# A linear-attention plus SwiGLU block on one core: 384 instead of 512 tokens in the conventional part, preparation of the weights laid out anew

## The chip, the core and the metric

The kernel runs on one core of a Trainium2 chip. A core has TensorE (matmul, called PE; its weight loads are PEld), VectorE (DVE), ScalarE (ACT), GpSimd (POOL) and SyncE (SP, which issues DMAs here). They run side by side and wait for each other with semaphores. SBUF is the working memory, PSUM (eight banks of 512 fp32 columns per partition) takes what TensorE writes. The metric is the device time of one execution in microseconds (us).

## The reference

```python
x  = A_x                                   # [1, 2048, 512], bf16
xn = layernorm(x)                          # no gain, no bias, eps 1e-5
# A: linear attention, 32 heads of 16
q, k, v = split(xn @ wqkv)                 # wqkv [512, 1536]
phi = lambda t: where(t > 0, t + 1, exp(t)) + 1e-6
kv  = sum_s phi(k)_s v_s^T                 # per head, 16 x 16
z   = sum_s phi(k)_s
o   = (phi(q) kv) / (phi(q) z + 1e-6)
A   = o @ wo                               # wo [512, 512]
# B: SwiGLU
B   = (silu(xn @ w_gate) * (xn @ w_up)) @ w_down   # F = 1792
out = x + A + B
```

## The kernel before

Tokens lie in 16 tiles of 128. The program is written as a list of operations in an order set by hand: each `K.add(engine, ...)` appends one operation with the keys it reads and writes, waits are worked out from the keys, and every engine runs its own operations in the order of the list. Nothing is reordered at run time, so a late operation holds up all that stands behind it on its engine.

**Stage 1, to 48.7 us.** Normalisation, transposition of xn into xnT (by DMA, `dmat`, L412; tiles 0 to 3 by TensorE), the projections of q and k (`proj`, L431), phi, and G = xn^T phi(k) accumulated in banks 0 to 3 (`gacc`, L480). The order is the long text in `run`, whose words are a letter for a step and a tile number: D is `dmat`, q and k are projections. Behind it SP queues the loads of the gate, up, v, output and down weights. GpSimd then adds up z over 16 tiles (`z_add`, L497).

**Stage 2, conventional part, 48.7 to 74.7 us.** For the first `T0` = 512 tokens, 14 steps of gate and up (`gu`, L556): eight matmuls of 512 columns each, Silu on ScalarE (L564), the multiplication on VectorE (`hop`, L593). In step 2 the products of G with the v weights go in between (L605). Beside it the seven-product stage is prepared: the sum of squares of each weight matrix is bounded (`square` on ScalarE, L708 and, for w_down, `square_d`, L753; `top`, a maximum on VectorE, L714), turned into a power of two (`gather`, `total`, `scales`), with which `scale` multiplies the weights (ScalarE L800, GpSimd L801). `x_sum` and `w_sums` (both L808) form sums of blocks of xnT and of the weights in fp16.

**Stage 3, seven-product part, 74.7 to 154.0 us.** For the other 1536 tokens gate and up together are a product of 2 x 2 blocks, done with seven block products instead of eight (Winograd's form of Strassen's scheme). An iteration handles one of 14 blocks of 128 of F, for two halves q of `TS` = 384 columns: `prod` (L846) issues two matmuls per product and half; `seed` and `keep5` copy a bank (ScalarE, L856, L861); `gate` is Silu (L868); `u4` and `up22` combine (VectorE, L874, L879); `h22` (GpSimd, L883) and `h21` (VectorE, L889) write the result. `fill` puts matmuls of the conventional down projection of tiles 0 to 3 in between, 72 in all, FA and FB of them at two places of an iteration. Beside it go the scales and sums of the next weights, and per iteration one tile's division by the attention's denominator (`pz_mul`, `den_sum`, `den_turn`, `pq_mul`) and its transposition by DMA (`turn`).

**Stage 4, 154.0 us to the end.** The down projection and the attention output of 12 tiles in six pairs (`PAIRS`), again with seven products (`dprod`, L1083; `attn`, L1089), copies by `hcopy` (L1055), sums by `h_sum` (L1067), outputs by `dout` (L1115) and stores on SP.

Of the kernel before, what the change touches and what calls it, by code (L numbers as in the profile page):

```python
# [40 lines left out]
class _Program:  # L41
# [8 lines left out]
    def add(self, eng, fns, r=(), w=(), dma=False, a=()):  # L50
# [7 lines left out]
        for k in tuple(w) + tuple(a):  # L58
            if k in self.last_w:
                deps.add(self.last_w[k])  # L60
            deps |= self.readers.get(k, set())
        keep = []
        for d in deps:
            o = self.ops[d]
            if o["eng"] == eng and not o["dma"]:
# [52 lines left out]
def bass_parallel_sum__linear_attn_block__swiglu_ffn__prompt_kernel(nc, A_x, A_wqkv, A_wo, B_x, B_w_gate, B_w_up, B_w_down, out):  # L118
# [5 lines left out]
    with contextlib.ExitStack() as es:  # L124
# [17 lines left out]
        wg = sb("wg", [P, NDC, F], bf)  # L142
        wu = sb("wu", [P, NDC, F], bf)
# [38 lines left out]
        pqf = pq[:, :, :].rearrange("p a b -> p (a b)")  # L182
        wqf = wqkv[:, :, :].rearrange("p c f -> p (c f)").bitcast(f16)
# [18 lines left out]
        iw = sb("iw", [P, 2], f32)  # L202
        junks = [b_[:, :, :].rearrange("p a b -> p (a b)").bitcast(bf)[:, 0:F // 2] for b_ in (p5, c22)]
# [10 lines left out]
        banks = [E(nc.psum_tensor("pb%d" % i, [P, 512], f32)) for i in range(8)]  # L214
# [68 lines left out]

        blockmask(("maskt",), maskt[:, :], maskt[:, :].rearrange("p (a b) -> p a b", a=HPG), [[0, DH]])
# [128 lines left out]
        def dmat(t):  # L413
            K.add("sp", lambda e: e.dma_start_transpose(out=xnT[:, :, t * P:(t + 1) * P], in_=xn[:, t, :]),
                  r=[("xn", t)], w=[("xnT", t)], dma=True)

# [100 lines left out]
        def run(text):  # L517
# [11 lines left out]
            S6 m15 q10 x12 D14 s15 m12 k10 y10 s12 n10 k11 D0 x10 u10 R7 m10 q15 x11 s10 q11 m11 y15 L7 R6 s11  # L529
            D7 n15 k13 y11 u15 q13 n11 x13 L6 u11 D6 m13 q14 y13 s13 n13 q12 y14 u13 n14 k14 y12 u14 n12 q7  # L530
            x14 u12 m14 k7 y7 L1 s14 D1 n7 k6 x7 u0 m7 q6 u7 x6 s7 m6 G4 y6 s6 n6 G12 u2 G14 u6 u1 G6 u8 G10
            u3 G11 G15 G8 G13 G7
        """)
        fload("sp", "wg", wg, B_w_gate, 0)
        fload("sp", "wu", wu, B_w_up, 0)
        wload("sp", 2)
        woload("sp")

        for h in (1,):
            fload("sp", "wg", wg, B_w_gate, h)  # L540
            fload("sp", "wu", wu, B_w_up, h)
# [7 lines left out]
        def gu(j, extra=(), er=(), ew=()):  # L549
            C, fc = j // NFC, j % NFC  # L550
            n = (len(extra) + 7) // 8
            todo = list(extra)
            for b, w_, key in ((gb(j), wg, "wg"), (gb(j) + 1, wu, "wu")):
                fns = []
                for c in range(NDC):
                    fns.append(lambda e, c=c, b=b, w_=w_: e.matmul(  # L556
                        banks[b][:, :], w_[:, c, fc * P:(fc + 1) * P], xnT[:, c, C * 512:(C + 1) * 512],
# [4 lines left out]
                      r=sum([xkeys(t) for t in range(4 * C, 4 * C + 4)], []) + [(key, fc // 7), (key + "c", fc)] + list(er),  # L562
                      w=[B(b)] + list(ew))
            K.add("act", lambda e: e.activation(sil[:, j % 2, :], banks[gb(j)][:, :], ACT.Silu),  # L564
                  r=[B(gb(j))], w=[("sil", j % 2)])

        def h0(fc):
            return xn[:, 10 + fc, :] if fc < 6 else pk[:, 2 + fc, :]

        def h0key(fc):  # L570
            return ("xn", 10 + fc) if fc < 6 else ("pk", 2 + fc)

        HB = 2 * TB

        def hj(fc):
            if fc < 9:
                return hTf[:, fc * HB:(fc + 1) * HB]
            return xnf[:, (fc - 9) * HB:(fc - 8) * HB] if fc < 12 else pqf[:, (fc - 12) * HB:(fc - 11) * HB]

        def hjold(fc):  # L580
            if fc < 9:
                return ph1
            if fc < 12:
                return [("xn", t) for t in range(3 * (fc - 9), 3 * (fc - 8))]
            return [("pq", t) for t in range(3 * (fc - 12), 3 * (fc - 11))]

        def htile(t, fc):
            if t < 4:
                return h0(fc)[:, t * P:(t + 1) * P], h0key(fc)
            return hj(fc)[:, (t - 4) * P:(t - 3) * P], ("hj", fc, (t - 4) // 3)  # L590

        def hop(j):
            K.add("dve", lambda e: e.tensor_tensor(  # L593
                out=h0(j), in0=banks[gb(j) + 1][:, :], in1=sil[:, j % 2, :], op=ALU.mult),
                r=[B(gb(j) + 1), ("sil", j % 2)], w=[h0key(j)])
# [82 lines left out]
        def ounits(bank, t):  # L678
            out = []
            for fc in range(NFC):  # L680
# [3 lines left out]
                    start=(fc == 0 and t < 2), stop=(fc == NFC - 1 and t > 1))), [k_, ("wd", 7 * (fc // 7))], [B(bank)]))  # L684
# [10 lines left out]
        def oout(bank, t, home=None):  # L695
            dst = out_sb[:, t % 2, :] if home is None else home
            keys = [("ob", t % 2, 0), ("ob", t % 2, HD)] if home is None else [("ob", t)]
            K.add("dve", lambda e: e.tensor_tensor(out=dst, in0=banks[bank][:, :], in1=x_sb[:, t, :], op=ALU.add),
                  r=[B(bank)] + xk(t), w=keys, a=() if home is None else [("T", 4)])
# [37 lines left out]
        def scales(b):  # L737
# [6 lines left out]
                r=[B(b)], w=[B(b)])  # L744
            K.add("dve", lambda e: e.tensor_scalar(
                out=sw[:, :], in0=r_, scalar1=2.0 ** (SB - 65), scalar2=None, op0=ALU.mult), r=[B(b)], w=[("sw",)])
            K.add("dve", lambda e: e.tensor_scalar(
                out=iw[:, :], in0=e_, scalar1=2.0 ** (64 - SB), scalar2=None, op0=ALU.mult), r=[B(b)], w=[("iw",)])
            K.add("dve", lambda e: e.tensor_scalar(
                out=sx[:, :], in0=sw[:, 0:1], scalar1=2.0 ** SX, scalar2=None, op0=ALU.mult), r=[("sw",)], w=[("sx",)])  # L750
# [14 lines left out]
        def total_d(b):  # L765
# [4 lines left out]
        def scales_d(b):  # L770
# [583 lines left out]
```

## Time and profile before

| | us |
|---|---|
| three runs | 295.39, 200.62, 201.09 |
| median of them | 201.09 |
| profiled execution, its own time | 200.89 |
| its span, first to last instruction | 199.6 |

| engine | busy us | share of the span |
|---|---|---|
| TensorE | 195.1 | 98% |
| TensorE weight loads | 114.8 | 58% |
| VectorE | 170.5 | 85% |
| ScalarE | 153.6 | 77% |
| GpSimd | 122.3 | 61% |

The page gives busy time per engine, the chain of work that ended last, groups of instructions (line, engine, operation, written tile, read tiles, shape, count, then busy time, mean ns of one, and idle time before them with what ended it) and DMA queues. A line named in a group is that of the helper that issues it. Busy TensorE time is not peak time: matmuls overlap, so a matmul's pace is read from how many of them a stretch of the chain holds. The granted TensorE clock was 1.00 throughout.

### The profile page before, as it was taken

Reading aid. Unit: us, or ns where it says so; the run is one execution under the profiler, and the core shown is the slowest. Engines: PE = TensorE matmul, PEld = TensorE weight load, DVE = VectorE, ACT = ScalarE, POOL = GpSimd, SP = SyncE. Lnnn points to the kernel's source line nnn. Section 1 sums busy time; section 2 is a strip of 40 time slices with the busy share of each in tenths; the row PEclk is TensorE's granted clock in tenths of the full one; section 3 lists DMA queues with packets and bytes.
Section 4 is the critical chain, followed back from the end, with each engine's and each line's share of the span. In section 5 each row is a group of like instructions: output and inputs, shape, how many; then the busy total and the mean of one; then the engine's idle time right before and its main releaser. Section 6 shows DMA issues by size and latency. Waiting matters only on the chain.

```text
span 199.6 us, 3566 instructions
## 1 busy us (share of the span) xinstructions
PE 195.1 (98%) x1193; PEld 114.8 (58%) x1207; DVE 170.5 (85%) x339; ACT 153.6 (77%) x308; POOL 122.3 (61%) x150
## 2 busy tenths in 40 slices
PE   8899999999999999999999999999999999999995
PEld 2344444444544445555555555555555888888884
DVE  2999998894797798988888998887799999998866
ACT  3799887749889988689898988888989968475200
POOL 3687876799995544787677666768877004413220
DMA  6943243289990000011111221000210012132223
GB/s 180 355 122 81 57 87 73 50 282 364 375 295 3 0 3 0 0 28 31 26 26 26 53 56 23 4 0 7 45 34 0 3 39 66 30 79 66 45 69 118
DMA packets 28899, 15.97 MB, mean 80 GB/s; under 512 B 17232, under 2 KB 28880, under 8 KB 28880
## 3 DMA queue, kind: packets, MB, share of 16 engines
q1 hardware_dynamic: 28320, 15.28, 27.3%
q10 hardware_dynamic: 560, 0.46, 0.7%
q8 instruction: 9, 0.15, 0.3%
q14 instruction: 10, 0.08, 0.1%
HBM read 9.70 MB, written 2.10 MB: 59 GB/s over the span
## 4 chain that ended last, share of the span: by engine, by line
PE 94%; DVE 2%; DMA 2%; issue 1%; ACT 0%; POOL 0%; SPq 0%
PE pb L846 32%; PE pb L1083 16%; PE pb L431 13%; PE pb L556 12%; PE pb L480 7%; PE pb L682 6%; PE pb L1089 5%; PE pb L686 2%; DMA x_sb<-in_A_x_dram 2%; PE pb L605 1%; PE pb L674 0%; DVE pq L470 0%; PE pb L398 0%; POOL ef L459 0%; DVE stats L298 0%
## 5 line engine op out<-in xcount | busy, mean ns | idle before, releaser
L654 POOL TENSOR_TENSOR pq<-pq,rden 128x512 bf16<-128x512 bf16 x16 | 16.9, 1056 | 36.7 <-DVE rden L650 23.1
L868 ACT ACTIVATE zacc<-pb,iw 128x384 bf16<-128x384 f32 x56 | 31.3, 590 | 5.9 <-PE pb L846 4.7
L431 PE MATMUL pb<-wqkv,xnT 128*128 128x512 bf16 x110 | 25.1, 379 | 0.2
L846 PE MATMUL pb<-xnT,wg 128*128 128x384 bf16 x112 | 25.1, 326 | 0.0
L638 POOL TENSOR_TENSOR pz<-pq,zbc 128x512 f32<-128x512 bf16 x16 | 18.6, 1164 | 5.3 <-DVE ef L808 3.8
L883 POOL TENSOR_TENSOR hT<-c,zacc 128x384 bf16<-128x384 f32 x18 | 16.1, 915 | 6.0 <-DVE c L879 4.0
L459 POOL TENSOR_SCALAR ef<-ef 128x512 bf16<-128x512 bf16 x25 | 15.5, 620 | 5.8 <-ACT ef L452 5.6
L879 DVE TENSOR_TENSOR c<-pb,p 128x384 f32<-128x384 f32 x28 | 15.5, 555 | 4.1 <-PE pb L846 2.8
L431 PEld LDWEIGHTS pb<-wqkv,xnT 128*128 128x128 bf16 x112 | 10.9, 98 | 13.3 <-DVE pk L470 0.4
L452 ACT ACTIVATE ef<-pb 128x512 bf16<-128x512 f32 x25 | 14.8, 593 | 3.9 <-PE pb L431 3.9
L874 DVE TENSOR_TENSOR pb<-pb,p 128x384 f32<-128x384 f32 x28 | 15.3, 561 | 1.7 <-PE pb L846 0.9
L497 POOL TENSOR_TENSOR zacc<-zacc,pk 128x512 f32<-128x512 f32 x13 | 15.4, 1181 | 1.0
L856 ACT ACTIVATE pb<-pb 128x384 f32<-128x384 f32 x28 | 12.7, 473 | 3.8 <-PE pb L846 2.9
L846 PEld LDWEIGHTS pb<-xnT,wg 128*128 128x128 bf16 x112 | 10.6, 98 | 7.7 <-ACT pb L856 0.8
L556 PE MATMUL pb<-xnT,wg 128*128 128x512 bf16 x56 | 14.7, 379 | 0.0
L556 PE MATMUL pb<-xnT,wu 128*128 128x512 bf16 x53 | 14.3, 379 | 0.1
L846 PE MATMUL pb<-xnT,wqkv 128*128 128x384 bf16 x56 | 13.7, 326 | 0.0
L846 PE MATMUL pb<-GT,wqkv 128*128 128x384 f16 x56 | 13.7, 326 | 0.0
L846 PE MATMUL pb<-wo,wqkv 128*128 128x384 f16 x56 | 13.7, 326 | 0.0
L298 DVE BATCH_NORM_STATS2 stats<-x_sb 128x6 f32<-128x512 bf16 x16 | 10.8, 678 | 3.0 <-DMA x_sb<-in_A_x_dram 3.0
L1089 PE MATMUL pb<-M,pk 128*128 128x256 bf16 x96 | 13.4, 273 | 0.0
L480 PE MATMUL pb<-pk,xn 128*128 128x512 bf16 x55 | 12.5, 379 | 0.1
(210 smaller groups left out, 488.6 us busy)
## 6 DMA issues: line engine op xcount, KB each, us to landing
x_sb<-in_A_x_dram SPq DMA_DIRECT2D x14, 128.0 KB, 4.5
wg<-in_B_w_gate_dram SPq DMA_DIRECT2D x2, 896.0 KB, 8.3
wu<-in_B_w_up_dram SPq DMA_DIRECT2D x2, 896.0 KB, 9.6
wd<-in_B_w_down_dram SPq DMA_DIRECT2D x2, 896.0 KB, 13.7
out_dram<-out_sb SPq DMA_DIRECT2D x24, 64.0 KB, 1.6
wqkv<-in_A_wqkv_dram SPq DMA_DIRECT2D x3, 256.0 KB, 5.0
wqkv<-in_A_wqkv_dram SPq DMA_DIRECT2D x1, 512.0 KB, 9.0
wo<-in_A_wo_dram SPq DMA_DIRECT2D x1, 512.0 KB, 10.0
```

The source lines that it names most:

```text
L431: K.add("pe", [(lambda e, c=c: e.matmul(banks[b][:, :], src[:, c, t * P:(t + 1) * P], wqkv[:, c, col:col + D], start=(c == 0), stop=(c == ...
L459: K.add("pool", lambda e: e.tensor_scalar(out=buf, in0=buf, scalar1=top, scalar2=0.0, op0=ALU.min, op1=ALU.max), r=[bkey] + tkeys, w=[bkey])
L480: K.add("pe", [(lambda e, c=c: e.matmul(banks[c][:, :], src[:, t, c * P:(c + 1) * P], pk[:, t, :], start=first, stop=last)) for c in range ...
L556: fns.append(lambda e, c=c, b=b, w_=w_: e.matmul(banks[b][:, :], w_[:, c, fc * P:(fc + 1) * P], xnT[:, c, C * 512:(C + 1) * 512], start=(c ...
L638: K.add("pool", lambda e: e.tensor_tensor(out=pzh[i][:, :, 0:DH], in0=heads(pq[:, t, :]), in1=heads(zbc[:, :]), op=ALU.mult), r=[("pq", t) ...
L654: K.add("pool", lambda e: e.tensor_tensor(out=heads(pq[:, t, :]), in0=heads(pq[:, t, :]), in1=rden[:, i, :][:, :, None].broadcast_to([P, N ...
L846: K.add("pe", [(lambda e, c=c: e.matmul(banks[bank][:, 0:TS], L[i][:, c, :], R[i][:, c, ts], start=(start and c == 0), stop=(c == 1), skip ...
L868: K.add("act", lambda e: e.activation(sil4[:, n, :], bk(bank), ACT.Silu, scale=iw[:, 0:1]), r=[B(bank), ("iw",)], w=[("sil4", n), ("zacc", ...
L879: K.add("dve", lambda e: e.tensor_tensor(out=c22[:, q, :], in0=bk(b), in1=p5[:, q, :], op=ALU.add), r=[B(b), ("p5", q)], w=[("c22", q)])
L883: K.add("pool", lambda e: e.tensor_tensor(out=hj(fc)[:, TB + q * TS:TB + (q + 1) * TS], in0=c22[:, q, :], in1=sil4[:, 2 * q + 1, :], op=AL ...
L1083: K.add("pe", [(lambda e, k=k: e.matmul(split(banks[b][:, 0:HD]), L[:, k, :], cut[:, :, k * P:(k + 1) * P], start=(start and k == 0), stop ...
L1089: K.add("pe", [(lambda e, g=g: e.matmul(dk(b), pk[:, SLOT[t], g * P:(g + 1) * P], M[:, g, lo:lo + HD], start=False, stop=(g == NG - 1), sk ...
```

## The change

- `T0` is 384: the conventional part takes three tiles with matmuls of 384 columns; the seven-product part has 1664 tokens in halves of 416 columns. Buffers that lie in freed memory (`h0`, `hj`) move accordingly. Tile 3 goes through the seven-product gate and up, but its down projection stays among the 72 fill matmuls; its scale is undone by one more ScalarE copy on `rden` (in `den_turn`) and in `oout`.
- The first half of the gate weights is queued on SP behind the transposition of tile 14, the first half of the up weights behind that of tile 6; the transposition of tile 0 stands just ahead of that of tile 1. The second gate half comes first of the other loads, the second up half behind wo.
- The preparation is two texts in the manner of `run`: `AHEAD` (seven squares, one maximum, the G evictions, x_sum 1) before the first gate/up step, and `BESIDE`, by step 0 to 13 of the conventional part, and from 14 on by half iterations of the seven-product part. Three w_down squares stay beside the conventional part; five, and w_down's scale, are in the iterations. The scales of the first and third pair of up blocks move to ScalarE.
- The gate's factor is negative. All sums with gate weights become additions, so `w_sums` forms S0 and S2 with one VectorE instruction of 1024 columns (a repeated operand and a backward step over one joined tensor `wgu`), and the copies, `u4`, `up22` change sign.
- Banks of the two halves are (4, 2, 6) and (5, 3, 7). Fill matmuls per iteration come from a table `FILLS`.
- Token order of the divisions and the pairs is nearly the natural one. In the last pair the fourth product of the down projection is issued behind two attention parts instead of ahead of them.

```diff
-T0 = 512
+T0 = 384
-ORDER = (0, 1, 2, 3, 4, 5, 10, 11, 12, 13, 14, 15, 6, 7, 9, 8)
+ORDER = tuple(range(14)) + (15, 14)
-PAIRS = (10, 4, 12, 14, 6, 8)
+PAIRS = (4, 6, 8, 10, 12, 14)
...
         def dmat(t):
...
+            if t == LG:
+                fload("sp", "wg", wg, B_w_gate, 0)
+            if t == LU:
+                fload("sp", "wu", wu, B_w_up, 0)
...
-            S6 m15 q10 x12 D14 s15 m12 k10 y10 s12 n10 k11 D0 x10 u10 R7 m10 q15 x11 s10 q11 m11 y15 L7 R6 s11
+            S6 m15 q10 x12 D14 s15 m12 k10 y10 s12 n10 k11 x10 u10 R7 m10 q15 x11 s10 q11 m11 y15 L7 R6 s11
...
-            x14 u12 m14 k7 y7 L1 s14 D1 n7 k6 x7 u0 m7 q6 u7 x6 s7 m6 G4 y6 s6 n6 G12 u2 G14 u6 u1 G6 u8 G10
+            x14 u12 m14 k7 y7 L1 s14 D0 D1 n7 k6 x7 u0 m7 q6 u7 x6 s7 m6 G4 y6 s6 n6 G12 u2 G14 u6 u1 G6 u8 G10
...
-        fload("sp", "wg", wg, B_w_gate, 0)
-        fload("sp", "wu", wu, B_w_up, 0)
+        fload("sp", "wg", wg, B_w_gate, 1)
         wload("sp", 2)
         woload("sp")
-
-        for h in (1,):
-            fload("sp", "wg", wg, B_w_gate, h)
-            fload("sp", "wu", wu, B_w_up, h)
+        fload("sp", "wu", wu, B_w_up, 1)
...
+            if t == C0:
+                K.add("act", lambda e: e.activation(rden[:, i, :], rden[:, i, :], ACT.Copy, scale=sw[:, 1:2]),
+                      r=[("rden", i), ("sw",)], w=[("rden", i)])
...
             if part == 0:
-                tt("dve", S_[0], A21, A22, ALU.add, uk, [("S", n, 0)] + old)
-                tt("dve", S_[1], S_[0], A11, ALU.subtract, gk + [("S", n, 0)], [("S", n, 1)])
+                both = Sw[:, n, 0:3:2, :, :]
+                lhs = A21[:, None, :, :].broadcast_to([P, 2, 2, 2 * P])
+                tt("dve", both, lhs, wgu[:, :, cs].rearrange("p (x c) f -> p x c f", c=2)[:, 3::-3, :, :], ALU.add,
+                   gk + uk, [("S", n, 0), ("S", n, 2)] + old)
             else:
-                tt("dve", S_[2], A11, A21, ALU.subtract, gk + uk, [("S", n, 2)])
-                tt("dve", S_[3], A12, S_[1], ALU.subtract, gk + [("S", n, 1)], [("S", n, 3)])
-
-        GB = ((2, 3, 4), (5, 6, 7))
+                tt("dve", S_[1], S_[0], A11, ALU.add, gk + [("S", n, 0)], [("S", n, 1)])
+                tt("dve", S_[3], A12, S_[1], ALU.add, gk + [("S", n, 1)], [("S", n, 3)])
+
+        GB = ((4, 2, 6), (5, 3, 7))
...
+        AHEAD = "q130 q000 q110 q120 q030 t010 G00 q021 G30 q020 G21 G11 X1"
+        BESIDE = {0: "q101 t100", 2: "t001 q011 q131 k", 4: "t121 m0 m1 t031 d5", 6: "q111 u012 u045 u078 u101 u167 g m2", 8: "T C m3 X3 d1", 9: "a10", 11: "p00 W0 d7 W1 Z2", 12: "z0", 13: "X2 a12 z1 p11 p01 X4", 14: "d6 d3", 18: "d4", 21: "d0", 22: "d2", 27: "h", 28: "D e", 29: "s0", 30: "s1", 32: "s2 s3", 33: "s4 s5"}
...
-        FA, FB = 2, 3
-        DIV = {i: ORDER[i] for i in range(11)}
-        TURN = {11: (8, 9), 12: (10,)}
+        FILLS = ((3, 4), (2, 3), (1, 3), (3, 5), (1, 4), (1, 2), (0, 2), (2, 2), (1, 3), (1, 3), (1, 3), (1, 2), (3, 3), (6, 1))
+        DIV = {i + 0: ORDER[i] for i in range(11)}
...
         oout(1, 3, spare[1])
         dprod(p, 3, e, False)
-        dprod(p, 4, b, False)
         attn(p, 0, HD, e)
         dout(p, 0, HD, e)
         attn(p, 0, 0, a)
         dout(p, 0, 0, a)
+        dprod(p, 4, b, False)
         attn(p, 1, 0, b)
         dout(p, 1, 0, b)
```

In the two texts q is a square, t a maximum, G an eviction of G, X an x_sum, W a half of w_sums, a and p a scale on ScalarE or GpSimd, d a square of w_down, z a denominator product, Z the total of z; k, m, T, C, g, h, D, e, s and u are the small steps in between.

More of the change, by code (lines that the diff above doesn't have):

```diff
@@ L213, in bass_parallel_sum__linear_attn_block__swiglu_ffn__prompt_kernel @@
         sm = sb("sm", [P, 1], f32)
-        banks = [E(nc.psum_tensor("pb%d" % i, [P, 512], f32)) for i in range(8)]
+        psum = E(nc.psum_tensor("pb", [P, 8, 512], f32))
+        banks = [psum[:, i, :] for i in range(8)]
         def B(i):
@@ L561, in gu @@
                 K.add("pe", fns,
-                      r=sum([xkeys(t) for t in range(4 * C, 4 * C + 4)], []) + [(key, fc // 7), (key + "c", fc)] + list(er),
+                      r=sum([xkeys(t) for t in range(C0)], []) + [(key, fc // 7), (key + "c", fc)] + list(er),
                       w=[B(b)] + list(ew))
-            K.add("act", lambda e: e.activation(sil[:, j % 2, :], banks[gb(j)][:, :], ACT.Silu),
+            K.add("act", lambda e: e.activation(sil[:, j % 2, 0:T0], banks[gb(j)][:, 0:T0], ACT.Silu),
@@ L763, in gather_d, with total_d @@
                 r=[("as1",)], w=[("as1b",)])
-        def total_d(b):
+        where_d = []
+        def total_d():
+            where_d.append([b for b in (1, 0) if not busy.get(B(b))][0])
+            b = where_d[0]
             one = nc.const_aps.tensor(1.0, (P, P), bf)
@@ L898, in fill @@
                 K.add("pe", fn, r=r, w=w)
+                busy[w[0]] = after is None
                 if after is not None:
```

269 lines of the change are left out of this document (120 added, 149 removed).

## The prediction

> **What bounds the kernel now.** I read the page first (parts 1, 2 and 4), then busy time by stage, the groups by shape, the waits, and the timeline around the stage borders.
>
> ```profile
> span 199.6 us, 3566 instructions
> ...
> PE 195.1 (98%) x1193; PEld 114.8 (58%) x1207; DVE 170.5 (85%) x339; ACT 153.6 (77%) x308; POOL 122.3 (61%) x150
> ...
> PE 94%; DVE 2%; DMA 2%; issue 1%; ACT 0%; POOL 0%; SPq 0%
> ```
>
> TensorE is busy for 98% of the span and carries 94% of the chain that ended last. Busy is not yet peak, so I checked the pace: in the chain 21 matmuls of 512 columns take 4.53 us, 20 of 384 take 3.25 and 28 of 256 take 3.06: 0.2157, 0.1624 and 0.109 us each, that is columns / 2.4 GHz plus about 2 ns, at a granted clock of 1.00. By stage:
>
> ```profile
> 48.70:74.70 26.00, 25.84 (x132) 12.25 (x133) 21.36 (x39) 23.77 (x50) 18.66 (x16) 1.00 0.44 147
> 74.70:153.99 79.29, 78.93 (x456) 44.14 (x462) 69.63 (x143) 69.19 (x136) 57.70 (x58) 1.00 0.10 23
> 153.99:199.60 45.61, 43.48 (x395) 37.81 (x392) 39.43 (x79) 23.92 (x34) 9.65 (x10) 1.00 0.21 56
> ```
>
> The columns are window, length, then busy PE, PEld, DVE, ACT, POOL. Conventional part: 112 x 0.2157 + 16 x 0.056 (kv) + 5 x 0.2157 = 26.1, measured 26.0. Seven-product part: 392 x 0.1624 + 69 fill matmuls x 0.2157 = 78.5, measured 79.3. So nothing but TensorE's column count is on the path, and at most 0.8 us of stalls can be removed there. That bounds the gain from above.
>
> **The change, part by part.**
>
> *Columns.* The conventional part loses 112 x (0.2157 - 0.1624) = 5.97 us. Seven products then run over 416 columns instead of 384; 416 is not in the trace; between the rows of 384 and 512 it lies between 0.162 and 0.216, by the pace at 0.1757: 392 x 0.0133 = 5.23 us added. The fills stay 72 matmuls. Net **-0.74 us**. This is the only sure gain.
>
> *Preparation beside a shorter part.* The conventional part falls from 26.0 to 20.1 us (112 x 0.1624 + 0.9 + 1.1), with 1.30 us per gate/up step. ScalarE's load there was 23.8 us. Now: two G evictions 1.1, 14 Silu of 384 at about 0.48 (612 ns at 512 less 128 columns at 0.95 ns) 6.7, four squares and three of w_down at 0.94 pitch 6.6, four M copies 2.2, zbc 0.65, two scales 2.3, floors 0.6: 20.2 us, full to the brim. Seven squares moved ahead need 7 x 0.94 = 6.6 us from the table load's end at 42.0 to 48.6, just where the G evictions may start (48.75 now). Walking the queue step by step, the gate/up step 12 finds its banks free by 0.1 us, and the first seed copy (behind the last scale and the floor copy, 70.35 to 70.8) ends just as its product arrives (70.85). Hidden, but with no slack: I take 0; the ends are -0.1 and +1.5 (each 1% on ScalarE's queue costs 0.2 us once the slack is gone).
>
> *x_sum 1 before the first product step.* On VectorE it now stands ahead of the first gate/up multiplication, beside GpSimd's z additions (1181 ns each, up to 62.95).
>
> ```profile
> L808 DVE TENSOR_TENSOR wqkv<-xnT,GT 128x1536 f16<-128x1536 bf16 x1 | 1.5, 1500 | 0.0
> ...
> L808 DVE TENSOR_TENSOR wo<-xnT 128x1536 f16<-128x1536 bf16 x1 | 0.9, 947 | 0.0
> ```
>
> The columns are busy time, mean ns of one, idle before. The first row ran beside a GpSimd scale (75.26 to 76.38), the second beside an idle GpSimd: 1.58 times as long. For 1664 columns that is 1.03 to 1.63; I take 1.63, the row nearest in kind. It ends at 51.7, the multiplication at 52.25, and step 2's up half wants that bank at 52.25: **+0.07**.
>
> *ScalarE in the seven-product part.* Five squares of w_down move into it.
>
> ```profile
> L868 ACT ACTIVATE zacc<-pb,iw 128x384 bf16<-128x384 f32 x56 | 31.3, 590 | 5.9 <-PE pb L846 4.7
> ...
> L856 ACT ACTIVATE pb<-pb 128x384 f32<-128x384 f32 x28 | 12.7, 473 | 3.8 <-PE pb L846 2.9 <-DVE hT L889 0.7
> ...
> L753 ACT ACTIVATE xs<-wd 128x896 bf16<-128x896 bf16 x8 | 7.8, 975 | 0.0
> ...
> L800 ACT ACTIVATE wg<-wg,sw 128x1024 bf16<-128x1024 bf16 x5 | 5.7, 1138 | 0.0
> ```
>
> An iteration has four gates, two seeds, two keeps: 4 x 31.3/56 + 2 x 12.7/28 + 2 x 12.2/28 (the keeps' row, L861) = 4.02, with 32 more columns at 0.95 ns on eight instructions 4.26. Iterations 2 to 4 add a scale (1.14) and a square (0.975) each, iteration 3 also the new copy on rden (0.25, as the 128x32 floor copy; it waits for VectorE's reciprocal, with the second gates queued behind it and GpSimd's division waiting for it): 6.37 + 6.62 + 6.37 = 19.4. TensorE has 28 x 0.1757 = 4.92 plus 4, 8 and 5 fills: 5.78 + 6.65 + 6.00 = 18.4. So ScalarE is 0.9 behind after iteration 4; a seed may be some 0.4 late (ready 1.0 us after the iteration starts, wanted at 1.4), and iterations 5 to 8 give back a little. Bounds 0 (back-to-back gates have a pitch of 0.535, not 0.559, and then the sums meet) and 0.9; I take **+0.3**, which also covers iteration 6 with no fill ahead of product 3 (u4 ready 0.81 after product 6, wanted at 0.70).
>
> *Two sums in one VectorE instruction.* Separate: 0.42 each (414 to 426 ns for 512 columns). The slope between 512 and 1536 columns (421 and 951 ns) gives 0.69 for 1024; with a repeated row and a backward step this form is not in the trace, and one column per cycle, as in the 896-column maximum (1075 ns), gives 1.23. VectorE was busy 5.0 of 5.6 us per iteration; either is covered: 0, and the upper end is a rival below. Negated signs change operands, not counts; the tiny constants cost four GpSimd memsets beside the first loads (GpSimd idle there): 0.
>
> *Loads.* The first gate half is queued on SP behind transposition 14 (issued 28.52), ahead of 7 (32.12); the first up half behind 6.
>
> ```profile
> 33.85 1.19 SPq L414 DMA_TRANSPOSE xnT<-xn  x1
> 38.16 1.19 SPq L414 DMA_TRANSPOSE xnT<-xn  x1
> 39.40 0.58 SPq L221 DMA_DIRECT2D wg<-in_B_w_gate_dram  x1
> ```
>
> That load was waited for until 44.50, 5.1 us after issue. Issued at 29.8 it lands at 34.9, and tile 7 (2.4 us alone: 34.5) at up to 36.0 if it stands behind it; its projection is the fourth from the end (39.91 - 4 x 0.86 = 36.5). Hidden by 0.5 us: 0. If its 2.4 us only begin at 34.9, it is there at 37.3: +0.85. Later loads move up; the second up half lands near 49.7, its first square starts at 50.3.
>
> *Border to the down projection.* The first pair is now tokens 512 to 767 instead of 1280 to 1535, so its last copy waits for h21 of iteration 13 (VectorE, after the last product) instead of h22.
>
> ```profile
> 154.12 0.72 ACT L1055 ACTIVATE xn<-pq,sx 128x512 bf16<-128x512 bf16 x1
> ...
> 154.87 0.62 DVE L1067 TENSOR_TENSOR xn<-wqkv,xn 128x896 f16<-128x896 bf16 x1
> ```
>
> The copy ended at 154.84, the sum behind it at 155.49. Now the first h21 (started 153.80) ends at 154.34, a copy of 768 (924 ns) at 155.3, the sum at 155.95; the product that reads it starts at 155.84: **+0.17** (0 to 0.5).
>
> *Last pair.* The chain's end stays: last attention matmul, 0.48 of VectorE, store, 1.6 us landing; outputs ahead of it were not waited for. 0 to -0.15. Attention of the last tile is 0.77 earlier: its transposition, issued 192.40, lands near 194.8, wanted at 195.23. Cover 0.4; without it up to +0.77. I take 0.
>
> Sum: -0.74 + 0.07 + 0.30 + 0.17 = -0.20 on the profiled execution's 200.89 (span 199.6): **200.7 us**. The median shown, 201.09, is of 200.62, 201.09 and one run of 295; the two near each other average 200.86, so the profiled time is their like. A measurement tells about 2% of this kernel from no change, 4 us.
>
> **Rivals.**
> 1. All of it hidden: 200.89 - 0.74 = 200.15, to 199.9 with the tail. For it: ScalarE was 5.00 busy of 5.00 us from 60 to 70 without a TensorE stall, so a full queue needn't cost. Chance 0.22.
> 2. The port that VectorE and GpSimd share. If x_sum 1 must wait out a whole z addition, it ends at 50.0 + 1.18 + 1.03 = 52.25, the multiplication at 52.8, and step 2 stalls 0.6 instead of 0.07: 201.3. For it: 1500 against 947 ns; against: the same sum beside another GpSimd scale took 981 (GpSimd paid, 1.89 us). Chance 0.10. The Trainium skill, "SBUF — State Buffer", Who interferes with whom, says that a VectorE instruction with two SBUF inputs and a GpSimd one that reads SBUF exclude each other for a whole instruction, whoever starts first; it speaks against putting x_sum 1 there, and by it the sum would be 201.3. The two rows agree.
> 3. Slower: ScalarE's backlog. In the old iterations ScalarE reached 5.09 of 5.6 us, 91%. If that is a ceiling, since its instructions wait for each product in turn, iterations 2 to 4 need 19.4 / 0.91 = 21.3: +2.9 instead of +0.3, 203.3; if it lasts through iterations 5 to 9 (28.1 / 0.91 against 28.3) +2.6 more, 205.9. It decides once a seed is over 0.4 late. Against: rival 1's row. Chance 0.20, with 0.13 up to 204.9 and 0.07 above.
> 4. The merged sum does not save. At 1.23 it delays the next u4 by 0.4 in each of seven pairs; VectorE's 0.6 us of idle time hides all or, where two fills or fewer stand by, half of it: 200.9 to 202.1. Chance 0.05. The Trainium skill, "VectorE: DVE Perf Modes", What auto-detection actually checks, gives two results a cycle where all operands are 16-bit with step +1 or -1, which holds for the innermost step here; no run here shows this form yet.
>
> **Numbers.** Forecast 200.7 with its own range 200.3 to 201.0: 0.40. Unnamed causes 0.03. The range 199.9 to 203.0 leaves out about 0.15 (most of rival 3 beyond 203). Faster by 2% (below 196.9) would need stalls that aren't there: 0.01. Slower by 2% (above 204.9): 0.07 + 0.02. Within: 0.90.
>
> **What would show it.** Products of 416 at 0.176 pitch; the conventional part about 20.1 us, the seven-product part about 84; ScalarE near 100% in iterations 2 to 4 with TensorE waiting for a seed (rival 3) or not (1); the wait of TensorE before step 2's up half; the merged sum at 0.69 or 1.2; no gap before tile 7's projection at 36.5 nor before the last attention. Wrong would be a stall over 1 us anywhere, or a pace above 0.176.

## The result and the profile after

The changed kernel takes 201.62 us (median of 22 runs), the kernel before 200.64 beside it: ratio 1.005, 95% interval 1.0034 to 1.0067. Measured once more, beside one of the experiments, it took 201.32 against 200.80: 1.0031, 1.0019 to 1.0043. So it is 0.5 to 1.0 us slower, where 0.2 us faster was forecast. The time lies in the wide range of the forecast (199.9 to 203.0) and outside its narrow one (200.3 to 201.0); the sign is wrong.

The profiled execution has a time of its own of 201.90 us, 1.01 above the one of before. The page of the kernel after, its span, busy time and the chain by engine:

```profile
span 200.6 us, 3559 instructions
...
PE 195.4 (97%) x1193; PEld 114.7 (57%) x1207; DVE 173.6 (87%) x333; ACT 157.1 (78%) x313; POOL 124.2 (62%) x152
...
PE 86%; DVE 5%; DMA 3%; ACT 1%; issue 1%; POOL 1%; SPq 0%
```

Before, TensorE carried 94% of that chain. Now 8 points have gone to VectorE, a DMA and others: TensorE is waiting for something at places where it waited for nothing. Not all of the detour through other engines is loss: a chain that reaches TensorE through a transposition goes back along it as far as it was late.

The three stages of the kernel after; the columns are window, length, then busy time of PE, PEld, DVE, ACT and POOL:

```profile
48.79:69.77 20.98, 20.25 (x133) 12.29 (x134) 19.52 (x37) 17.48 (x39) 16.89 (x14) 1.00 0.31 101
69.77:154.50 84.73, 84.24 (x457) 44.01 (x463) 73.69 (x137) 76.21 (x147) 61.48 (x60) 1.00 0.10 21
154.50:200.60 46.10, 43.69 (x393) 37.53 (x391) 39.19 (x78) 23.92 (x33) 9.38 (x9) 1.00 0.22 56
```

These windows begin where the first matmul of a stage stands in the chain. By the same marks (48.71, 74.88 and 154.16, the last two some 0.17 us later than the rounder windows of the prediction) the stages of before were 26.17, 79.28 and 45.44 us. That gives the account:

| | before | after | difference | forecast |
|---|---|---|---|---|
| start of the conventional part | 48.71 | 48.79 | +0.08 | 0 |
| conventional part | 26.17 | 20.98 | -5.19 | -5.97 + 0.07 + 0 |
| seven-product part | 79.28 | 84.73 | +5.45 | +5.23 + 0.30 |
| down projection to the end | 45.44 | 46.10 | +0.66 | +0.17 + 0 |
| sum | | | +1.00 | -0.20 |

Two rows are off: the conventional part gave 0.71 us less than forecast, the last stage cost 0.49 more. What TensorE's matmuls waited for in the kernel after (engine, line and what it waited for; then us in total, times, longest) names a place in each:

```profile
PE pb L758 <- DVE as2b L752: 0.6, 1, 0.6
...
PE pb L1090 <- DMA pk<-pq: 0.3, 1, 0.3
```

L758 (`total`) is one matmul of two columns that adds up the bound on the weights' squares over the partitions. It stands in TensorE's queue ahead of the next down-projection and gate/up work, and reads what VectorE's `gather` (L752) clamps. L1090 is the attention of the last tile, which reads the transposition of that tile.

### The profile page after: what moved, and what is told of

Read it like the earlier page. It is cut to its first block, busy times and chain, and to the rows that moved or that the text cites. A ratio compares the mean times of both kernels' runs of the same rounds, so it can differ in the third digit from the quotient of the medians.

```text
span 200.6 us, 3559 instructions
## 1 busy us (share of the span) xinstructions
PE 195.4 (97%) x1193; PEld 114.7 (57%) x1207; DVE 173.6 (87%) x333; ACT 157.1 (78%) x313; POOL 124.2 (62%) x152
## 4 chain that ended last, share of the span: by engine, by line
PE 86%; DVE 5%; DMA 3%; ACT 1%; issue 1%; POOL 1%; SPq 0%
PE pb L876 35%; PE pb L1084 13%; PE pb L443 13%; PE pb L492 7%; PE pb L564 7%; PE pb L704 5%; PE pb L1090 5%; DMA x_sb<-in_A_x_dram 2%; DMA pk<-pq 2%; PE pb L708 2%; DVE xnT L1068 1%; DVE asum L746 1%; DVE out_sb L1116 1%; POOL pq L676 1%; ACT xs L777 1%
## 5 line engine op out<-in xcount | busy, mean ns | idle before, releaser
L876 PE MATMUL pb<-xnT,wgu 128*128 128x416 bf16 x112 | 26.5, 339 | 0.0
L906 ACT ACTIVATE zacc<-pb,iw 128x416 bf16<-128x416 f32 x28 | 16.6, 612 | 4.4 <-PE pb L876 3.5
L564 PE MATMUL pb<-xnT,wgu 128*128 128x384 bf16 x112 | 19.9, 326 | 0.1
L916 DVE TENSOR_TENSOR c<-pb,p 128x416 f32<-128x416 f32 x28 | 16.4, 589 | 3.9 <-PE pb L876 1.9
L920 POOL TENSOR_TENSOR hT<-c,zacc 128x416 bf16<-128x416 f32 x16 | 15.3, 974 | 6.7 <-DVE c L916 4.1
L911 DVE TENSOR_TENSOR pb<-p,pb 128x416 f32<-128x416 f32 x28 | 16.3, 593 | 2.1 <-PE pb L876 0.8
L876 PEld LDWEIGHTS pb<-xnT,wgu 128*128 128x128 bf16 x112 | 10.9, 98 | 8.8 <-ACT pb L886 0.3
L901 ACT ACTIVATE zacc<-pb,iw 128x416 bf16<-128x416 f32 x28 | 15.7, 626 | 0.0
L564 PEld LDWEIGHTS pb<-xnT,wgu 128*128 128x128 bf16 x112 | 10.9, 98 | 7.0
L1084 PE MATMUL pb<-wgu,xnT 128*128 128x256 f16 (+1 forms) x112 | 14.9, 273 | 0.0
L876 PE MATMUL pb<-xnT,wqkv 128*128 128x416 bf16 x56 | 14.4, 339 | 0.2
L876 PE MATMUL pb<-wo,wqkv 128*128 128x416 f16 x56 | 14.4, 339 | 0.0
L876 PE MATMUL pb<-GT,wqkv 128*128 128x416 f16 x56 | 14.4, 339 | 0.0
L1090 PE MATMUL pb<-M,pk 128*128 128x256 bf16 x96 | 13.6, 273 | 0.3 <-DMA pk<-pq 0.3
```

Source lines behind the costliest of these rows:

```text
L564: fns.append(lambda e, c=c, b=b, w_=w_: e.matmul(banks[b][:, 0:T0], w_[:, c, fc * P:(fc + 1) * P], xnT[:, c, 0:T0], start=(c == 0), stop=( ...
L876: K.add("pe", [(lambda e, c=c: e.matmul(banks[bank][:, 0:TS], L[i][:, c, :], R[i][:, c, ts], start=(start and c == 0), stop=(c == 1), skip ...
L901: K.add("act", lambda e: e.activation(sil4[:, q, :], bk(a), ACT.Silu, scale=iw[:, 0:1]), r=[B(a), ("iw",)], w=[("sil4", q)], a=[("zacc", 0 ...
L906: K.add("act", lambda e: e.activation(sil4[:, 2 + q, :], bk(d), ACT.Silu, scale=iw[:, 0:1]), r=[B(d), ("iw",)], w=[("sil4", 2 + q)], a=[(" ...
L911: K.add("dve", lambda e: e.tensor_tensor(out=bk(d), in0=p5[:, q, :], in1=bk(b), op=ALU.subtract), r=[B(b), ("p5", q)], w=[B(d)])
L916: K.add("dve", lambda e: e.tensor_tensor(out=c22[:, q, :], in0=bk(b), in1=p5[:, q, :], op=ALU.subtract), r=[B(b), ("p5", q)], w=[("c22", q)])
```

## Where the conventional part lost its 0.8 us

The timeline of the kernel after, around `gather`; the columns are start, length (first start to last end of a row), engine, line, operation:

```profile
59.80 1.46 DVE L746 TENSOR_TENSOR asum<-asum 128x1 f32<-128x1 f32 x5
...
61.30 0.17 DVE L749 TENSOR_REDUCE as<-asum 128x2 f32<-128x16 f32 x1
...
61.50 1.00 DVE L752 TENSOR_SCALAR as2b<-as 128x2 bf16<-128x2 f32 x1
...
62.65 0.16 PE L758 MATMUL pb<-as2b,const-bfloat16-1.0 128*128 128x2 bf16 x1 [0.62 <-DVE as2b L752]
```

The same three steps in the kernel before:

```profile
65.02 0.29 DVE L722 TENSOR_TENSOR asum<-asum 128x2 f32<-128x2 f32 x3
65.35 0.17 DVE L725 TENSOR_REDUCE as<-asum 128x2 f32<-128x16 f32 x1
...
65.55 0.17 DVE L728 TENSOR_SCALAR as2b<-as 128x2 bf16<-128x2 f32 x1
...
66.73 2.29 POOL L638 TENSOR_TENSOR pz<-pq,zbc 128x512 f32<-128x512 bf16 x2 [3.77 <-DVE ef L808]
```

The clamp of the same two columns took 0.17 us then and 1.00 us now; the squarings 0.29 (three of one to three columns) and 1.46 (five of one column). Nothing in these instructions explains a microsecond. The instructions on GpSimd do: before, GpSimd was idle here (for 3.77 us up to 66.73, the last row); after, the z additions are under way. The lines for single durations (min/median/max in ns, first and last start) of the kernel after:

```profile
L746 DVE TENSOR_TENSOR asum<-asum x5: 146/147/1117, 59.8 to 60.1; 128x1 f32<-128x1 f32 x5
```
```profile
L509 POOL TENSOR_TENSOR zacc<-zacc,pk x4: 1151/1157/1171, 57.6 to 61.3; 128x512 f32<-128x512 f32 x4
```

Four squarings took about 0.15 to 0.21 us and one took 1.117, a whole z addition less a little. By the starts of the additions, one ran from 60.08 to about 61.25, and the long squaring ended at 61.26; the next ran from 61.32 to 62.47, and the clamp ended at 62.50. The matmul L758 followed at 62.65, 0.62 us late, with all later TensorE work behind it.

So this is the mechanism of rival 2, but at another place than the one it was given. x_sum 1, where the prediction looked for it, did wait:

```profile
L837 DVE TENSOR_TENSOR ef<-xnT 128x1664 f16<-128x1664 bf16 x1 | 1.5, 1539 | 0.0
...
L837 DVE TENSOR_TENSOR wo<-xnT 128x1664 f16<-128x1664 bf16 x1 | 1.0, 1016 | 0.0
```

1.54 us beside the additions, and 1.02 for a later one of the same size (at 64.00) that began together with a GpSimd scale, which then took 2.01 us: there it was GpSimd that waited. The forecast had 1.63 for the first. But no TensorE instruction waited for it, in this profile or the others. The Trainium skill, "SBUF — State Buffer", Who interferes with whom, states the rule behind both places: a VectorE instruction with two SBUF inputs, or one of the kinds that use both ports, and a GpSimd instruction that reads SBUF exclude each other for a whole instruction. The ends above agree with it to 0.03 us. What counts here is easily passed over: the wait is for a whole addition, however short the waiting instruction, so that one of a single column took 1117 ns instead of 147.

## Experiments

Three runs tell apart what made L758 late: theory A, the port that VectorE and GpSimd share; theory B, ScalarE's queue, late by a late load.

**The gather's small instructions on one column, with one tensor input.** The arithmetic stays the same. The squarings take their second factor as a scalar per partition; the clamp, which had one tensor input already, becomes two instructions of one column:

```diff
-            K.add("dve", lambda e: e.tensor_tensor(out=v, in0=v, in1=v, op=ALU.mult), r=ks, w=ks)
+            K.add("dve", lambda e: e.tensor_scalar(out=v, in0=v, scalar1=v, scalar2=None, op0=ALU.mult), r=ks, w=ks)
...
-            K.add("dve", lambda e: e.tensor_scalar(
-                out=as2b[:, :], in0=as2[:, :], scalar1=2.0 ** -60, scalar2=2.0 ** 80, op0=ALU.max, op1=ALU.min),
+            for i in (0, 1):
+                K.add("dve", lambda e, i=i: e.tensor_scalar(
+                    out=as2b[:, i:i + 1], in0=as2[:, i:i + 1], scalar1=2.0 ** -60, scalar2=2.0 ** 80, op0=ALU.max, op1=ALU.min),
```

> The five squarings of single columns take their second factor as a per-partition scalar instead of a second tensor, and the clamp of the two sums is two one-column instructions; nothing else differs from the changed kernel, where the five squarings took 1.46 us and the clamp 1.00 us (0.29 and 0.17 us before), both beside GpSimd's z additions. Theory A, the port that VectorE and GpSimd share: these instructions drop to about 0.5 and 0.3 us, the sum over partitions no longer waits 0.62 us on TensorE, the conventional part falls from 21.0 to about 20.3 us, the time by 0.4 to 0.6 us. Theory B, ScalarE's queue (the second up half landed late, at 51.6): the clamp comes at most 0.3 us earlier and the conventional part stays within 0.2 us of 21.0.

Measured: 200.81 us, ratio to before 1.000 (0.998 to 1.002). The timeline of this run:

```profile
59.73 0.69 DVE L747 TENSOR_SCALAR asum<-asum 128x1 f32<-128x1 f32 x5
...
60.45 0.17 DVE L750 TENSOR_REDUCE as<-asum 128x2 f32<-128x16 f32 x1
60.66 0.22 DVE L754 TENSOR_SCALAR as2b<-as 128x1 bf16<-128x1 f32 x2
...
61.80 0.17 PE L760 MATMUL pb<-as2b,const-bfloat16-1.0 128*128 128x2 bf16 x1
```

GpSimd's additions run on as before, 1.46 + 1.00 us have become 0.69 + 0.22, TensorE's wait is gone, and its stage:

```profile
48.72:68.92 20.20, 20.10 (x134) 12.36 (x134) 18.27 (x38) 17.51 (x40) 16.73 (x14) 1.00 0.32 104
```

20.20 against 20.98 us. The new form is no faster by itself (0.20 us a squaring against 0.147 without interference); it is only not held up. At the clamp the number of columns alone made the difference: 1.00 us for the instruction on two, 0.15 for each of the two on one. 26.17 - 20.20 is 5.97, the number worked out for the columns, to the digit.

**The other side: fewer z additions.** Those of tiles 5 to 14 are left out, so that GpSimd is idle beside the gather, whose instructions stay as they were.

```diff
-        for t in range(1, NT):
+        for t in (1, 2, 3, 4, NT - 1):
```

> Left out: the z additions of tiles 5 to 14 on GpSimd (the denominator is then wrong, the work behind it is the same). GpSimd is idle from about 50 us on in the conventional part. Theory A: x_sum 1 takes 1.03 us instead of 1.54, the five squarings 0.3 us, the clamp 0.17 us, the wait of the sum over partitions is gone, the conventional part is 20.2 to 20.4 us. Theory B: x_sum 1 gets shorter, but the wait stays at about 0.6 us, because ScalarE's squares and copies decide when the sums are complete.

Measured: 200.74 us, ratio 0.999 (0.997 to 1.001). The old forms, undisturbed:

```profile
60.16 0.42 DVE L746 TENSOR_TENSOR asum<-asum 128x1 f32<-128x1 f32 x5
...
60.82 0.17 DVE L752 TENSOR_SCALAR as2b<-as 128x2 bf16<-128x2 f32 x1
```

Either taking the instruction out of the clash or taking the partner out removes the same wait. The stage was 20.63 us here and not 20.20: the second up half landed at 52.0 in this execution, ScalarE waited 2 us for it, and TensorE waited 0.2 to 0.4 us for ScalarE's and VectorE's results. x_sum 1 still took 1.54 us, where the expectation had 1.03: the addition of tile 15, which stays, ran beside it (49.30 to 50.46).

**Loads in another order.** The second up half goes ahead of wo on SP, since in the kernel after it took 10.3 us to land (issued 41.20, there at 51.5), and ScalarE's square waited 1.32 us for it.

```diff
-        woload("sp")
         fload("sp", "wu", wu, B_w_up, 1)
+        woload("sp")
```

> The second up half is queued ahead of wo instead of behind it; nothing else differs from the changed kernel. ScalarE's wait of 1.3 us for that load ends (it lands about 1.4 us earlier). Theory B, ScalarE's queue: everything behind it on ScalarE moves up by 1.3 us, step 5's multiplication with it, the wait of the sum over partitions goes, the conventional part falls to about 20.3 us. Theory A, the shared port: the squarings start earlier but still wait for the z additions; the clamp moves up by about the same 1.3 us less what the port takes, so that the wait may shrink too; it tells A from B only by the lengths of the squarings and the clamp, which stay near 1.5 and 1.0 us under A and need not under B.

Measured: 201.36 us, ratio 1.0034 (1.0013 to 1.0054). ScalarE's wait is gone, and L758 waits as before:

```profile
59.37 1.46 DVE L746 TENSOR_TENSOR asum<-asum 128x1 f32<-128x1 f32 x5
...
61.07 1.00 DVE L752 TENSOR_SCALAR as2b<-as 128x2 bf16<-128x2 f32 x1
62.22 0.16 PE L758 MATMUL pb<-as2b,const-bfloat16-1.0 128*128 128x2 bf16 x1 [0.61 <-DVE as2b L752]
```

The stage took 20.98 us, the same. Theory B falls as the cause of this wait.

**The last pair's order.** The chain of the kernel after, its end (start, length, what):

```profile
191.93 1.07 POOL pq L676
193.00 0.02 issue
193.01 3.22 DMA pk<-pq
196.23 0.05 issue
196.28 1.05 PE pb L1090 x8
```

The transposition of the last tile landed after 3.22 us, the median of all sixteen being 2.4, and the attention could have followed the seven matmuls ahead of it at 195.84 (started 195.07, 0.11 us each): 0.44 us lost by the pace. The list of waits above gives 0.3, since it counts from the modelled end of the last matmul. Two runs change only this order, one undoing it in the changed kernel, one putting it into the kernel before.

```diff
         dprod(p, 3, e, False)
+        dprod(p, 4, b, False)
         attn(p, 0, HD, e)
         dout(p, 0, HD, e)
         attn(p, 0, 0, a)
         dout(p, 0, 0, a)
-        dprod(p, 4, b, False)
```

> Only the last pair's order is undone in the changed kernel: its third product stands ahead of the last tile's attention again, as in the kernel before. Theory A (the transposition is late, and the reorder took its cover away): TensorE's wait for it before the last attention (0.44 us in the changed kernel's profile, 0 to 0.54 in the profiles of the experiments so far) becomes 0, the tail is 0.1 to 0.5 shorter and the median 0.1 to 0.4 below the changed kernel's 201.62, that is 201.2 to 201.5. Theory B (the wait is hidden by the store that ends the kernel): the median stays within 0.1 of 201.62.

> Only the last pair's new order, put into the kernel before. The transposition of the last tile was issued at 192.40 there and must land 2.8 us later. Theory A: it lands after 2.4 to 3.4 us, so TensorE waits 0 to 0.6 us: ratio to the kernel before 1.000 to 1.002. Theory B (the reorder does some good at the end, since less stands behind the last attention): 0.1 us or more below the kernel before, ratio 0.9995 or less.

Measured: undone 201.13 us, ratio 1.0022 (1.0003 to 1.0041), that is 0.2 to 0.5 under the changed kernel's two medians; in the kernel before 200.90 against 200.62, ratio 1.0013 (0.9991 to 1.0035). The end of the chain with the order undone:

```profile
193.78 2.62 PE pb L1084 x24
196.40 1.32 PE pb L1090 x12
```

No wait is left, and the last stage is 45.76 us instead of 46.10. The kernel before with the new order:

```profile
191.98 3.06 DMA pk<-pq
195.04 0.05 issue
195.09 1.05 PE pb L1089 x8
```

Here TensorE lost 0.28 us by the same pace. The medians alone do not settle it: the interval of the second run holds 1, and that of the first overlaps those of the changed kernel. That the wait appears and goes with the order is what the two chains show. Among the profiles with the new order it was 0 to 0.70 us by the pace (0 to 0.54 counted as in the list of waits).

**Both repairs together.**

> The changed kernel with two edits together: the gather's squarings and clamps in one-column scalar form (which alone gave 200.81), and the last pair's order undone. Theory A (two separate losses, 0.8 at the small sum and 0.1 to 0.4 at the tail): 200.4 to 200.7, level with the kernel before or 0.1 to 0.2 us below it. Theory B (the tail costs nothing): 200.8 again.

Measured: 200.54 us, ratio 0.9987 (0.9969 to 1.0005). Against the changed kernel that is 0.8 to 1.1 us, which fits two separate losses that add up. The interval overlaps that of the gather's repair alone (200.81), but the stages show both: the conventional part of this run is 20.19 us long, and the last stage is 0.36 shorter than with the gather's repair alone (45.78 against 46.14).

**Fill matmuls of iteration 13.** At the end of the seven-product part the last product waited 0.53 us for VectorE's second `up22` (the PEld row of L876 at 153.97, on c L916). Two fill matmuls are moved within that iteration, from ahead of products 3 and 7 to ahead of product 4: `FILLS[13]` is (4, 3) instead of (6, 1), since the last products wait for `up22`, and fills ahead of them cover that wait. (The number of fills after the seven-product part stays 3; the wording of a later expectation, that two come there, is wrong in this.)

> In iteration 13 four fill matmuls stand ahead of product 3 and three behind product 7, instead of six and one; nothing else differs from the changed kernel. My theory: the last product waited 0.5 us for the second half's up22, because only one fill matmul stood before it; with three the wait goes, the seven-product part falls from 84.7 to about 84.2 us, the time by 0.3 to 0.5 us. Rival: product 3 then waits for u4 by as much as is gained, and the part stays at 84.7.

Measured: 201.54 us, ratio 1.0033 (1.0005 to 1.0061): no gain worth the name. The wait is gone and comes back 1.8 us later. The border to the down projection in this run:

```profile
153.43 1.09 DVE L926 TENSOR_TENSOR pq<-pb,zacc 128x416 bf16<-128x416 f32 x2 [0.41 <-PE pb L876]
...
154.06 0.94 ACT L1056 ACTIVATE xn<-pq,sx 128x768 bf16<-128x768 bf16 x1 [0.55 <-DVE pq L926]
...
154.90 0.36 ACT L1096 ACTIVATE pb<-pb 128x256 f32<-128x256 f32 x1
...
155.32 0.61 PE L1090 MATMUL pb<-M,pk 128*128 128x256 bf16 x4 [0.16 <-ACT pb L1096]
```

The copy of 768 columns waits for the last h21, the seed stands behind the copy on ScalarE, and the attention waits for the seed. From the first product of the seven-product part to this attention it is 86.01 us here (69.31 to 155.32) and 86.01 in the changed kernel (69.77 to 155.78): a stall taken out ahead of a chain that has none to spare moves to its end.

**The border eased.** With the fills as above and the two repairs, the copies of the first pair are cut so that only slice 13, 256 columns, is behind the last product; slices 8 to 10 are copied in iteration 12 and 11 and 12 in iteration 13, in gaps of ScalarE ahead of the second gates.

```diff
-        PIECE = ((0, 7), (7, 1), (8, 3), (11, 3))
+        PIECE = ((0, 7), (7, 1), (8, 3), (11, 3), (11, 2), (13, 1))
...
+            for i in {12: (2,), 13: (4,)}.get(fc, ()):
+                hcopy(0, i)
...
-            for i in {11: (1,), 12: (0,), 13: (2, 3)}.get(fc, ()):
+            for i in {11: (1,), 12: (0,), 13: (5,)}.get(fc, ()):
```

> As the run with both edits, and the border to the down projection eased: iteration 13 has two fill matmuls fewer ahead of its last products (they come behind the first product of the down projection), and the copies of the first pair's hidden rows are cut so that slices 8 to 10 are copied in iteration 12, 11 and 12 in iteration 13 ahead of the second gates, and only slice 13 (256 columns instead of 768) behind the last product. Theory A (the border's chain is last product, h21, copy of 768 columns, sum, product; 0.5 to 0.6 lost at up22 and 0.2 to 0.3 at the copy): the seven-product part is about 84.1 and the copy behind it 0.5 instead of 0.94; 0.3 to 0.8 us below the run with both edits, 199.8 to 200.2. Theory B (ScalarE is full in iterations 12 and 13, so the copies moved there make gates and seeds late): no gain or a loss up to 0.5 us.

Measured: 199.90 us, ratio 0.9959 (0.9941 to 0.9978), faster than both kernels. Its border and its stages:

```profile
153.83 0.51 ACT L1058 ACTIVATE xn<-pq,sx 128x256 bf16<-128x256 bf16 x1 [1.37 <-DVE pq L928]
...
154.32 0.37 ACT L1098 ACTIVATE pb<-pb 128x256 f32<-128x256 f32 x1
```
```profile
48.88:69.08 20.20, 20.20 (x135) 12.36 (x134) 18.36 (x38) 17.48 (x39) 16.74 (x14) 1.00 0.32 102
69.08:153.52 84.44, 84.44 (x464) 44.13 (x463) 73.43 (x137) 76.73 (x148) 61.59 (x60) 1.00 0.10 21
153.52:199.10 45.58, 43.43 (x393) 37.60 (x391) 39.41 (x79) 23.55 (x33) 9.27 (x9) 1.00 0.22 56
```

TensorE is busy for 20.20 of 20.20 and 84.44 of 84.44 us. From the first product to the first attention it is now 85.68 us, 0.33 less. The last stage is 0.20 us shorter than with the two repairs alone (45.58 against 45.78). Theory B, a ScalarE too full for the moved copies, falls.

**This version with the up half ahead of wo as well.**

> The run with the scalar forms, the old last pair and the eased border, with the second up half loaded ahead of the output weights in addition (the load order that alone gave 201.36 on the changed kernel, 0.26 below it, an amount within its interval). If a late second up half still costs something once the small sum's wait is gone: 0.1 to 0.3 below that run's 199.90, 199.6 to 199.8. If its cost was hidden: 199.9 again, within 0.1.

Measured: 199.90 us, ratio 0.995 (0.9932 to 0.9969): the same median, though on another chip, where the kernel before took 200.82 instead of 200.62; by the ratios it is 0.2 us less, within the intervals. That ScalarE's wait can be hidden is shown by the profile of the run before: the load landed at 51.6, ScalarE waited 1.3 us for it, and TensorE was busy throughout the conventional part. With a landing at 52.0, in the run with fewer z additions, it was not hidden.

**The merged sum taken apart**, alone in the changed kernel:

```diff
-                both = Sw[:, n, 0:3:2, :, :]
-                lhs = A21[:, None, :, :].broadcast_to([P, 2, 2, 2 * P])
-                tt("dve", both, lhs, wgu[:, :, cs].rearrange("p (x c) f -> p x c f", c=2)[:, 3::-3, :, :], ALU.add,
-                   gk + uk, [("S", n, 0), ("S", n, 2)] + old)
+                parts = wgu[:, :, cs].rearrange("p (x c) f -> p x c f", c=2)
+                for i, x in ((0, 3), (2, 0)):
+                    tt("dve", S_[i], A21, parts[:, x, :, :], ALU.add, gk + uk, [("S", n, i)] + old)
```

> The changed kernel with its merged weight sum written as two instructions of 512 columns each, nothing else changed. One theory (the merged sum, 0.68 us in the changed kernel, is covered by VectorE's idle time, and so would be two of 0.42): the median stays within 0.1 of 201.62 and the seven-product part stays at 84.7. The other (the sum stands on the path, and merging it saved 0.16 in each of seven pairs of iterations): up to 1.1 us slower, 202.1 to 202.7.

Measured: 201.16 us, ratio 1.0023 (1.000 to 1.0047). Neither theory had it below the changed kernel's 201.62. Its seven-product part, which holds the edit, is 84.78 us against 84.73. So the changed kernel and this one were run side by side on that chip:

> The changed kernel itself once more, on the same chip as the next run, because the run with the split sum came out 0.46 us below it though the stage that holds that edit had the same length. If the difference belongs to the chip or to when the first load and the last transposition land: near 201.2 here too, level with the next run within 0.15. If splitting the sum is worth something: 201.6 again, 0.3 or more above the next run.

> The changed kernel with the merged weight sum split in two, as in the earlier run, beside the changed kernel on the same chip. If the split is worth nothing: level with the run before within 0.15. If it is worth something: 0.3 or more below it.

Measured: 201.32 (1.0019 to 1.0043) and 201.11 (1.0013 to 1.0034). 0.30 of the 0.46 lies between the two measurements of the changed kernel itself; 0.21 is left on one chip, between the two expectations and with overlapping intervals. The profiles place it at the end: in both profiles of the split sum the last transposition landed after 2.4 us and was not waited for, in both of the changed kernel after 3.1 and 3.2, with 0.34 and 0.44 us lost. Whether the split has a part in that, the runs do not show. The stage of the edit shows no difference, so there the merge is worth nothing that can be measured. The rows of the merged form (kernel after) and of the two halves (this experiment), 714 ns against 2 x 433:

```profile
L837 DVE TENSOR_TENSOR wqkv<-wgu 128x1024 f16<-128x1024 bf16 x7 | 5.0, 714 | 0.0
```
```profile
L837 DVE TENSOR_TENSOR wqkv<-wgu 128x512 f16<-128x512 bf16 x14 | 5.5, 433 | 0.0
```

## Why the prediction was wrong, step by step

*Columns*: right. 20 products of 416 take 3.52 us in the chain, 0.1760 each against 0.1757. The conventional part fell by exactly 5.97 once the wait was out, and 392 x (0.1760 - 0.1624) is 5.33 for the other.

*Preparation beside a shorter part*: this is the step that failed. It walked ScalarE's queue alone, and took 0 with an upper end of 1.5. ScalarE was not what ended late; VectorE was: the matmul L758 waited 0.62 us for its `gather`, which the walk does not hold. The change of T0 and the new text `BESIDE` put the gather beside the z additions, where it had stood beside an idle GpSimd. The kernel before showed both halves of the price: the gather's rows of 0.15 to 0.17 us with GpSimd idle, and a GpSimd addition of 1.18. The prediction gave the additions (1181 ns each, up to 62.95) and looked for the clash at x_sum 1 alone; it did not ask what else on VectorE now falls beside them. Measured: +0.78 us in place of 0.

*x_sum 1*: the size was right (1.54 for 1.63), the stall of 0.07 did not come.

*ScalarE in the seven-product part*: +0.30 was too much. The three iterations with scales and squares (windows laid by the products and fills of each, so good to about 0.1 us):

```profile
82.90:88.70 5.80, 5.75 (x33) 3.09 (x33) 5.07 (x11) 5.54 (x13) 3.77 (x5) 1.00 0.11 24
88.70:95.30 6.60, 6.60 (x38) 3.47 (x37) 4.96 (x10) 6.04 (x12) 4.79 (x6) 1.00 0.11 24
95.30:101.30 6.00, 5.95 (x34) 3.17 (x34) 5.41 (x11) 6.00 (x13) 3.55 (x5) 1.00 0.11 22
```

ScalarE was busy for 17.57 of 18.40 us (the forecast's 19.4 adds up rows whose instructions overlap at their ends; a window counts such time once) and reached 6.00 of 6.00 in the last, with TensorE at work for 5.95 of them. The 91% that rival 3 took for a ceiling is none. The whole part grew by 5.45, of which 5.33 is columns: 0.12 for everything else.

*Two sums in one instruction*: 0.71 us against 0.69, covered, as forecast. Rival 4 falls.

*Loads*: tile 7's projection did not wait, as forecast. The second up half landed 1.8 us later than the 49.7 given. With the gather repaired this cost TensorE nothing; half a microsecond later still, at 52.0, it cost up to 0.4 us.

*Border to the down projection*: +0.17 was of the right size, but at another point. The product that reads the first sum did not wait. VectorE's sums came 0.28 us later than before, counted from the first product of the down projection (155.49 - 154.50 against 154.87 - 154.16), and this reached TensorE at 159.90, where a weight load waited 0.29 us for VectorE (L1110): 28 matmuls took 3.24 us there instead of 3.06. With the 0.34 of the last pair that is most of the last stage's +0.66. The eased border wins 0.33 us up to the first attention. Not all of that is a cost of the change: weight loads of the kernel before waited for the second `up22` and for the seed as well, by 0.28 and 0.30 us, against 0.53 and 0.36.

*Last pair*: this step failed too, by a term. Its "cover 0.4" took 2.4 us for the transposition, the median of the whole run, where 2.83 us were to be had. The profile of the kernel before already held the longer time; of its sixteen transpositions,

```profile
DMA to landing us min/median/max: 2.4/2.4/3.1
```

the longest is the last. Put into that kernel the new order met 3.06, in the changed kernel 3.22. The order undone wins 0.34 us in the last stage and 0.2 to 0.5 by the medians. The bound given for it, up to +0.77, was right; the value taken, 0, was not.

Of the rivals, the first (all hidden, 200.15) is not reached by the two repairs: 200.54 against 200.62 is -0.08, where the columns alone were put at -0.74. The -0.72 of the eased border (199.90) comes near that number by chance, since it also takes away waits that the kernel before had. The second had the mechanism, the price of a whole GpSimd instruction, and the wrong place; that its 201.3 is near the measured time is luck. So is the place of 201.62 in the wide range, whose upper end was set for ScalarE's backlog.

## What to carry to other kernels

When a step is moved, list for its new place what every engine that shares a resource with it is doing, and price the step by a row that has the same neighbour: the shortest instructions lose most, since a wait for a whole GpSimd instruction does not shrink with them. A cover is measured against the slowest of the like transfers at that point of the kernel, not against the median of all of them. And before a stall is taken out, follow the chain behind it: one that has no slack gives the gain back a little later.

## What the runs showed of the hardware that was not expected

- An instruction on one column (146 ns) took 1117 ns beside GpSimd additions of 1157 ns, and one on two columns 1002 instead of 172; the same arithmetic on one column with the second operand as a scalar took 0.20 us per instruction beside the same additions, and the clamp on one column 0.15, with no waiting to be seen.
- The exclusion goes both ways: GpSimd additions took 1154 ns, and 1820 the one (at 50.8) that met x_sum 1.
- DMA transpositions of one kind landed after 2.4 us in the median; the last of the kernel landed after 2.4 to 3.5 in the fourteen profiles, after 3.1 in the kernel before; a load of 896 KB queued behind others took 10.3 us, and 11.05 in another run.
- ScalarE was busy for all of a 6.0 us stretch (13 instructions, most of them behind a product) while TensorE was busy for 5.95 of it.
